# A fused attention and expert kernel in which the second dense product is folded into its neighbours

## The chip, the cores and the metric

The kernel runs on one core of a Trainium2 chip. The metric is the time of one execution in microseconds (us). A core has five engines that run side by side, each in the order of its own queue: TensorE (PE; its weight loads are listed apart as PEld), VectorE (DVE), ScalarE (ACT), GpSimd (POOL) and SyncE (SP), which here only issues transfers to the core's 16 DMA engines. ACT issues a few transfers too.

## What is computed

Attention with two head mixes gives `x` (1792 tokens x 768). Behind it stand a dense stage and a soft mixture of experts:

```python
h = x @ w_in                       # 1792 x 768 times 768 x 2048
g = h - np.tanh(h)
x = g @ w_out                      # 1792 x 2048 times 2048 x 768
logits = x @ phi                   # phi: 768 x 32 (8 experts, 4 slots each)
d = softmax(logits, axis=0)        # over the tokens
slot_input = (d.T @ x).reshape(8, 4, 768)
for e in range(8):
    slot_out[e] = np.maximum(slot_input[e] @ w1[e], 0.0) @ w2[e]   # w1: 768 x 1024, w2: 1024 x 768
c = softmax(logits, axis=1)
out = c @ slot_out
```

`w_in` and `w_out` come as 64-bit floats, all else in 32 bits. All large products run in a two-part form: an operand is split into a high part (`F32R`) and the rest, and hi*hi, lo*hi and hi*lo are added up.

## The kernel before, in words

The program is written in one order by hand (a manual schedule): each engine takes its instructions in the order in which the code issues them, and the waits follow from the data and from the buffers. `talking_heads` does the attention and, beside it, turns the 64-bit weights into 32 bits and stores them in DRAM, in 16 pieces `wi` and 16 pieces `wo` of 128 x 768. `moe_and_slots` is everything behind. Its first two products run beside the end of the attention.

Its main loop has 64 steps `t`, four batches `b` of 448 tokens times 16 slices `f` of 128 hidden units. Step `t` does

- `stage1` (L677): 18 matmuls of 128 x 448 into `hp`, slice `f` of `h` transposed (hidden units on the partitions);
- `gate`: three operations of ACT (L689 to L691) and six of DVE (L692 to L697) that make `g` of `hp`; `ready2` splits `g` (L645 on ACT, L646 on POOL or DVE);
- `stage2` (L710): 18 matmuls of 128 x 448 that add slice `f`'s share of `g @ w_out` to six banks `acc`, one or two steps later.

In batch 0 the weights come in one part and are split on the way: `split_to` makes the high part on ACT (L625) and the rest on POOL (L626), for `wi` and for `wo`; ACT's queue then stores both parts (`wis`, `wos`, 768 KB each). From batch 1 on both parts are loaded, 768 KB of `wis` and 768 KB of `wos` a step, into three and two buffers.

When `acc` of a batch is full, in the first four steps of the next one, the `prep_` functions copy it out (`x2T`), make the logits (L727), turn `x2T` by 24 transposes (L742), mix and exponentiate (L753, L756, L772) and add up the slots' inputs in `SA` (L821, L823). `sip` (L958) then gives the inputs `siT` of the experts. `hidden` (L980), `finish` (L997) and `slot_out` (L1008) run the eight experts from `w1` and `w2`; these come in 32 loads of 1536 KB (`ex`, L581) through SP's queue. SP issues them in the order of a list, each when a buffer of the list of free ones is there; a buffer comes back when PE has used it. The order ends with the second halves of `w2` of the experts 6 and 7. `slot_mix` and `output` (L1066) write the result.

Of the kernel before, what the change touches and what calls it, by code (L numbers as in the profile page):

```python
# [520 lines left out]
def moe_and_slots(tc, ident, xd, wi, wo, wis, wos, phi, w1, w2, out, box):  # L521
# [11 lines left out]
    LAG = 4  # L533
    LG = 3
    steps = [(b, f) for b in range(NB) for f in range(NF)]
    NST = len(steps)
# [4 lines left out]
    mids = ExitStack()
    firsts = ExitStack()
    keep = whole.enter_context(tc.tile_pool(name="m_keep", bufs=1))
    gp = mids.enter_context(tc.tile_pool(name="m_g", bufs=2, reuse_waits="tile"))
    temps = ExitStack()
    gt_p = temps.enter_context(tc.tile_pool(name="m_t", bufs=2, reuse_waits="tile"))
# [13 lines left out]
    queue += [4 * e + i for i in (2, 3) for e in (NE - 2, NE - 1)]  # L560

    def open_experts(stack, name, n, side):
        pool = stack.enter_context(tc.tile_pool(name=name, bufs=1, side=side, reuse_waits="tile"))
        for i in range(n):
            free.append((pool, f"{name}{i}"))

    def load_expert():
        if not queue or not free:
            return
        t = queue.pop(0)  # L570
        pool, tag = free.pop(0)
        e, part = divmod(t, 4)
        x = pool.tile([128, EXB], FP32, tag=tag, name="ex")
        i = part % 2
        if part < 2:
            n = KD // 2
            src = w1[e, i * n * 128:(i + 1) * n * 128, :]
        else:
            n = KF1
            src = w2[e, :, i * HALF:(i + 1) * HALF]  # L580
# [576 lines left out]
```

## Time and profile before

| | |
|---|---|
| median of 3 runs | 1144.0 us (1139.09 to 1148.11) |
| the profiled execution's own time | 1142.92 us |
| its span, first to last instruction | 1141.2 us |
| PE busy | 1078.0 us (94%) |
| DVE, ACT, POOL busy | 622.3, 556.4, 359.9 us |
| transfers | 274.35 MB, mean 240 GB/s |

The time of an execution is 1.7 us longer than the span of its trace. The busy share of an engine is a mean over stages that differ: in the attention, in the main loop and behind it different things come last, so the chain of what ended last (each piece followed back to what released it) and tables by stage tell more. Matmuls are pipelined: the trace gives one of 128 x 448 some 365 ns, but the next starts about 200 ns after it, so a run of them is read from start to start.

### The profile page before, as it was taken

The numbers are of one execution on the slowest core, as the hardware profiler recorded it, in microseconds if no ns is written. First come the engines' busy times: TensorE is split into PE (matmuls) and PEld (weight loads), VectorE is DVE, ScalarE is ACT, GpSimd is POOL, SyncE is SP. The second block draws the span as 40 slices with busy tenths as digits, with TensorE's granted clock in tenths as the row PEclk, the third lists the DMA queues.
The fourth block names the chain that finished last, engine by engine and source line by source line (L and its number), as shares of the span: only waits on it lengthen the run. The fifth ranks groups of instructions, "written<-read, shape, count | busy, mean of one in ns | idle before, by whom it ended". The sixth has DMA issues, their size and how long they took to land.

```text
span 1141.2 us, 20616 instructions
## 1 busy us (share of the span) xinstructions
PE 1078.0 (94%) x7400; PEld 865.1 (76%) x7400; DVE 622.3 (55%) x1330; ACT 556.4 (49%) x1245; POOL 359.9 (32%) x534
## 2 busy tenths in 40 slices
PE   8999999999989999989899999999999999998994
PEld 5677777777767777768777879997899979995452
DVE  3566576666756576645666774445634573444013
ACT  4776676766756677654344442333323342322022
POOL 1444455444634455554343301111121102110000
PEclk9999999999989999999989999999999999998999
DMA  5895678856875576447867846898465637948998
GB/s 127 236 248 172 189 217 236 225 170 181 236 211 168 180 225 218 166 165 258 293 267 277 318 166 231 302 405 326 165 236 212 238 139 271 389 170 305 379 388 310
DMA packets 158329, 274.35 MB, mean 240 GB/s; under 512 B 58292, under 2 KB 126964, under 8 KB 157716
## 3 DMA queue, kind: packets, MB, share of 16 engines
q1 hardware_dynamic: 153312, 247.76, 65.6%
q10 hardware_dynamic: 4868, 25.18, 5.5%
q8 instruction: 60, 0.98, 0.4%
q14 instruction: 41, 0.34, 0.1%
q0 software_dynamic: 48, 0.10, 0.0%
HBM read 185.71 MB, written 48.76 MB: 205 GB/s over the span
## 4 chain that ended last, share of the span: by engine, by line
PE 44%; DMA 3%; POOL 2%; issue 2%; ACT 2%; DVE 1%; ACTq 0%; POOLq 0%; SPq 0%; DVEq 0%
PE hp L677 18%; PE acc L710 18%; PE h L980 2%; PE so L1008 2%; DMA ex<-in_moe_w_dram 1%; DMA wo<-wos 1%; POOL wi L626 1%; PE tz L997 1%; POOL wo L626 1%; PE xtp L742 1%; PE lgp L727 1%; PE op L1066 1%; DMA xr<-xd 1%; ACT wi L625 1%; PE sp L821 1%
## 5 line engine op out<-in xcount | busy, mean ns | idle before, releaser
L677 PE MATMUL hp<-xh,wi 128*128 128x448 f32 x768 | 225.8, 374 | 14.2 <-POOL wi L626 9.7
L333 PEld LDWEIGHTS tm<-wk,e 120*112 120x112 f32 (+1 forms) x1440 | 176.6, 179 | 75.3 <-issue 59.6
L710 PE MATMUL acc<-gh,wo 128*128 128x448 f32 x768 | 218.5, 366 | 2.4 <-DMA wo<-wos 2.4
L299 DVE TENSOR_REDUCE mx<-pm 120x1 f32<-120x448 f32 x180 | 111.9, 622 | 138.1 <-PE pm L297 137.4
L333 PE MATMUL tm<-wk,e 120*112 120x120 f32 (+1 forms) x1440 | 179.4, 268 | 3.7 <-POOL wk L323 3.6
L297 PE MATMUL pm<-D,wpre 120*120 120x448 f32 x360 | 176.7, 573 | 1.8 <-ACT e L306 1.1
L323 POOL TENSOR_SCALAR wk<-wpost,rv 120x120 f32<-120x120 f32 x180 | 130.2, 723 | 142.1 <-PE tm L333 117.2
L677 PEld LDWEIGHTS hp<-xh,wi 128*128 128x128 f32 x768 | 145.3, 191 | 33.6 <-POOL wi L626 13.2
L336 ACT ACTIVATE aT<-tm 112x480 f32<-112x480 f32 x180 | 105.3, 585 | 125.4 <-PE tm L333 120.1
L646 POOL TENSOR_TENSOR gl<-g,gh 128x448 fp32r<-128x448 f32 x48 | 55.4, 1155 | 320.6 <-ACT gh L645 257.0
L710 PEld LDWEIGHTS acc<-gh,wo 128*128 128x128 f32 x768 | 144.0, 188 | 14.9 <-ACT xh L659 2.0
L692 DVE SCALAR_TENSOR_TENSOR qd<-qd,sq 128x448 f32<-128x448 f32 x64 | 47.2, 737 | 192.5 <-ACT qd L690 192.3
L677 PE MATMUL hp<-xl,wi 128*128 128x448 f32 x384 | 142.0, 370 | 1.3 <-DVE xl L660 1.3
L710 PE MATMUL acc<-gl,wo 128*128 128x448 f32 x384 | 140.3, 365 | 0.0
L306 ACT ACTIVATE e<-pm,mx 120x448 f32<-120x448 f32 x180 | 113.8, 632 | 4.9 <-DVE mx L299 2.6
L645 ACT ACTIVATE gh<-g 128x448 fp32r<-128x448 f32 x64 | 36.8, 576 | 138.4 <-DVE g L697 112.6
L275 ACT ACTIVATE S<-sc 120x448 f32<-120x448 f32 (+1 forms) x186 | 90.8, 544 | 13.4 <-PE sc L267 6.7
L351 PE MATMUL vx<-aT,vn 112*64 112x120 f32 (+1 forms) x1536 | 84.8, 264 | 5.2 <-DVE klo L234 5.0
L351 PEld LDWEIGHTS vx<-aT,vn 112*64 112x64 f32 x1536 | 74.9, 138 | 11.6 <-PE qx L247 6.2
L267 PE MATMUL sc<-khi,qT 64*120 64x448 f32 (+1 forms) x384 | 75.2, 385 | 6.5 <-DVE qT L251 6.1
L689 ACT ACTIVATE sq<-hp 128x448 f32<-128x448 f32 x64 | 34.5, 539 | 92.5 <-PE hp L677 72.8
L677 PEld LDWEIGHTS hp<-xl,wi 128*128 128x128 f32 x384 | 73.1, 190 | 7.8 <-DVE xl L660 2.0
(131 smaller groups left out, 1413.0 us busy)
## 6 DMA issues: line engine op xcount, KB each, us to landing
ex<-in_moe_w_dram SPq DMA_DIRECT2D x32, 1536.0 KB
wi<-wis SPq DMA_DIRECT2D x48, 768.0 KB
wo<-wos SPq DMA_DIRECT2D x48, 768.0 KB
D<-S SPq DMA_DIRECT2D x172, 210.0 KB
f<-in_moe_w_in_dram SPq DMA_DIRECT2D x32, 384.0 KB
f<-in_moe_w_out_dram SPq DMA_DIRECT2D x32, 384.0 KB
wis<-wi ACTq DMA_DIRECT2D x16, 768.0 KB
wos<-wo ACTq DMA_DIRECT2D x16, 768.0 KB
```

Source lines behind the costliest of these rows:

```text
L267: nc.tensor.matmul(xs[e][:ni], lhsT=qT[n][s, l, p, :ni], rhs=kt[s], start=(i == 0), stop=(i == 2))
L275: nc.scalar.activation(out=dst, in_=xs[e][:ni], func=ACTF.Copy)
L297: nc.tensor.matmul(x[:r], lhsT=wpre[:r, :m, :], rhs=D_t.pop(s)[:r], start=True, stop=True)
L299: nc.vector.tensor_reduce(out=mx[:r], in_=x[:r], op=ALU.max, axis=AX.X, negate=True)
L306: nc.scalar.activation(out=e[:r], in_=pp_t.pop(s)[:r], func=ACTF.Exp, bias=mx_t.pop(s)[:r], accum_out=ss[:r])
L323: nc.gpsimd.tensor_scalar(out=wk[:r], in0=wpost[:r], scalar1=ss_t.pop(s)[:r], scalar2=None, op0=ALU.mult)
L333: nc.tensor.matmul(x[:, c, :, :m], lhsT=e[:r, c * JP:(c + 1) * JP], rhs=wk[:r, :, :m], start=True, stop=True)
L336: nc.scalar.activation(out=attn_t[n][:, :, :, c0:c0 + m], in_=x[:, :, :, :m], func=ACTF.Copy)
L351: nc.tensor.matmul(x[64 * e:64 * e + 64, i, :ni], lhsT=nat_v[b, h // NP][:, h % NP, c, :], rhs=a[:, c, h, :ni], start=(c == 0), stop=(c == ...
L646: (nc.gpsimd if steps[t][0] else nc.vector).tensor_tensor(out=l, in0=src, in1=bits(h), op=ALU.subtract)
L677: nc.tensor.matmul(hp, lhsT=w[:, i, cs], rhs=x, start=(n == 0), stop=(n == 3 * KD - 1))
L710: nc.tensor.matmul(acc[c], lhsT=w[:, j, cs], rhs=g, start=(f == 0 and i == 0), stop=(f == NF - 1 and i == 2))
```

## The change

The product `g @ w_out` is no longer formed. The logits are `g @ (w_out @ phi)`, and the slots' inputs are `(d.T @ g) @ w_out`.

- `stage2`, the splitting of `g` and of `wo`, the store `wos` and its loads are gone, as are `x2T` and its transposes.
- In batch 0, each piece of `w_out` is loaded, turned by six transposes (`turn_w`), copied out by DVE and ACT, and multiplied by `phi` (`fold`, six matmuls of 32 columns), which gives a piece of `wphi`.
- In each step the slice of `g` made two steps before is turned by four transposes (`turn_g`) into a bank, and ACT copies it to a buffer by tokens. At every fourth step `logits` issues four matmuls (32 columns by 448) that add the last four slices' share.
- `gate` has a fourth operation on ACT (`mk`, for which DVE had the comparison L696) and five on DVE; `sq` now lies in PSUM. The gate of slice `t-1` is issued within the product of slice `t`, and the other pieces between the groups of three matmuls of a product (`hooks`).
- For each batch `slot_sum` makes `d.T @ g`, four groups of 512 columns, in the steps 4 to 7 of the next batch.
- Behind the loop 16 matmuls (`dt`) turn the sum over the batches, and 32 (`si`) multiply it by `w_out`, whose 16 pieces have been loaded again.
- The buffers are laid out anew. The loop's own ones leave room for 8 of the list's loads within the loop: the four loads of `w_out` (four pieces each) and the first two of `w1` in batch 1, two more of `w1` in batch 3. The other 28 loads of experts follow the loop.

```diff
...
+    def give(x, last=False):
+        free.append((x, last))
+        load_expert()
+    def load_expert():
+        if not queue or not free:
+            return
+        key = queue.pop(0)
+        home = free.pop(0)
+        x = home[0]
+        kind, t = key
+        if kind == "o":
+            for i in range(NG):
+                nc.sync.dma_start(out=x[:, i * DM:(i + 1) * DM], in_=wo[t * NG + i])
+        else:
+            e, part = divmod(t, 4)
+            i = part % 2
+            if part < 2:
+                n = KD // 2
+                src = w1[e, i * n * 128:(i + 1) * n * 128, :]
+            else:
+                n = KF1
+                src = w2[e, :, i * HALF:(i + 1) * HALF]
+            nc.sync.dma_start(
+                out=x.rearrange("p (a f) -> p a f", a=n), in_=src.rearrange("(a p) f -> p a f", p=128))
+        ex_tiles[key] = home
...
+    def load_w(t):
         if t < NST:
+            if t < NF:
+                nc.sync.dma_start(out=ring[t % 3][:, 1], in_=wi[t])
             else:
+                nc.sync.dma_start(out=ring[t % 3], in_=wis[t % NF])
+    def split_w(t):
         if t < NF:
+            w = ring[t % 3]
+            nc.scalar.activation(out=r32(w[:, 0]), in_=w[:, 1], func=ACTF.Copy)
+            nc.gpsimd.tensor_tensor(out=r32(w[:, 1]), in0=w[:, 1], in1=w[:, 0], op=ALU.subtract)
+    def save_w(t):
+        if t < NF:
+            nc.scalar.dma_start(out=wis[t], in_=ring[t % 3])
...
+    def product(t, hooks):
+        b, f = divmod(t, NF)
+        hp = bank(f"h{t % 3}", [128, SEQ], "hp")
+        w = r32(ring[t % 3])
         for c in range(KD):
+            for fn in hooks.get(c, []):
+                fn()
             cs = slice(c * 128, (c + 1) * 128)
+            for i, (hl, l) in enumerate(((0, 0), (1, 0), (0, 1))):
+                nc.tensor.matmul(
+                    hp, lhsT=w[:, hl, cs], rhs=r32(x_of(b, c, l)),
+                    start=(c == 0 and i == 0), stop=(c == KD - 1 and i == 2))
+        hps[t] = hp
+        for fn in hooks.get(KD, []):
+            fn()
+    def gate_act(t):
+        hp = hps[t]
+        qd, th, mk = mem["t"][GR:GR + 3]
+        sq = bank(f"q{t % 2}", [128, SEQ], "sq")
+        mem["sq"] = sq
         nc.scalar.activation(out=sq, in_=hp, func=ACTF.Square)
         nc.scalar.activation(out=qd, in_=sq, func=ACTF.Square, bias=tshift)
+        nc.scalar.activation(out=th, in_=hp, func=ACTF.Tanh)
+        nc.scalar.activation(out=mk, in_=sq, func=ACTF.Relu, bias=tlimit, scale=-1.0)
+    def gate_first(t):
+        hp, sq = hps[t], mem["sq"]
+        qd, th, mk = mem["t"][GR:GR + 3]
         nc.vector.scalar_tensor_tensor(out=qd, in0=qd, scalar=TG_E, in1=sq, op0=ALU.add, op1=ALU.mult)
+        nc.vector.tensor_tensor(out=mem["t"][t % GR], in0=hp, in1=th, op=ALU.subtract)
+        nc.vector.scalar_tensor_tensor(out=th, in0=sq, scalar=-TG_A, in1=qd, op0=ALU.add, op1=ALU.mult)
+    def gate_last(t):
+        hp = hps.pop(t)
+        qd, th, mk = mem["t"][GR:GR + 3]
+        nc.vector.scalar_tensor_tensor(out=hp, in0=th, scalar=TG_C, in1=hp, op0=ALU.mult, op1=ALU.mult)
+        nc.vector.copy_predicated(out=mem["t"][t % GR], mask=mk.bitcast(I32), data=hp)
...
-    def stage2(t):
...
-        for c in range(KD):
-            cs = slice(c * 128, (c + 1) * 128)
-            for i, (j, g) in enumerate(((0, gh), (1, gh), (0, gl))):
-                nc.tensor.matmul(
-                    acc[c], lhsT=w[:, j, cs], rhs=g, start=(f == 0 and i == 0), stop=(f == NF - 1 and i == 2))
...
+    turns = [0]
+    def turn_bank(shape, name):
+        turns[0] += 1
+        return bank(f"r{turns[0] % 2}", shape, name)
+    def turn_g(t):
+        b, f = divmod(t, NF)
+        if f % NG == 0:
+            tok[b, f // NG] = quads.pop(0)
+        g = mem["t"][t % GR]
+        x = turn_bank([JP, NR, 128], "gt")
+        for r in range(NR):
+            nc.tensor.transpose(out=x[:, r, :], in_=g[:, r * JP:(r + 1) * JP], identity=ident)
+        i = f % NG
+        dst = tok[b, f // NG][:JP].rearrange("p (r f) -> p r f", r=NR)[:, :, i * 128:(i + 1) * 128]
+        nc.scalar.activation(out=dst, in_=x, func=ACTF.Copy)
+    def load_o(f):
+        if f < NF:
+            nc.sync.dma_start(out=mem["wo"][f % 4], in_=wo[f])
+    def turn_w(f, hf):
+        x = turn_bank([128, HALF], "wt")
+        for i in range(KD // 2):
+            c = hf * (KD // 2) + i
+            nc.tensor.transpose(
+                out=x[:, i * 128:(i + 1) * 128], in_=mem["wo"][f % 4][:, c * 128:(c + 1) * 128], identity=ident)
+        dst = mem["wt"][f % 2][:, hf * HALF:(hf + 1) * HALF]
+        if hf:
+            nc.scalar.activation(out=dst, in_=x, func=ACTF.Copy)
+        else:
+            nc.vector.tensor_copy(out=dst, in_=x)
+    def fold(f):
+        x = turn_bank([128, NSL], "wp")
         for c in range(KD):
+            nc.tensor.matmul(
+                x, lhsT=mem["wt"][f % 2][:, c * 128:(c + 1) * 128], rhs=phs[:, c, :],
+                start=(c == 0), stop=(c == KD - 1))
+        nc.vector.tensor_copy(out=wphi[:, f, :], in_=x)
...
+    def logits(b, k):
+        if k == 0:
+            lg[b] = bank("lg", [128, SEQ], "lgp")
+        for g in range(NG):
+            f = k * NG + g
+            nc.tensor.matmul(
+                lg[b][NSL * g:NSL * g + NSL, :], lhsT=wphi[:, f, :], rhs=mem["t"][(b * NF + f) % GR],
+                start=(k == 0), stop=(k == NQ - 1))
...
+    def slot_sum(b, k, x):
+        a, es = es_in[b]
+        n = tok.pop((b, k))
+        for r in range(NR):
+            nc.tensor.matmul(
+                x[NSL * r:NSL * r + NSL, :], lhsT=es[:, r, :], rhs=n[:JP, r * FB:(r + 1) * FB], start=True, stop=True)
+        quads.append(n)
+        s = mem["SA"][:, k * FB:(k + 1) * FB]
+        if b:
+            nc.vector.scalar_tensor_tensor(out=s, in0=s, scalar=a, in1=x, op0=ALU.mult, op1=ALU.add)
+        else:
+            nc.vector.tensor_copy(out=s, in_=x)
+    folds = {}
+    for f in range(NF):
+        folds.setdefault(f + 3 if f < 2 else f + 2 if f < 7 else f + 1, []).append(f)
+    def step(t):
+        b, f = divmod(t, NF)
+        hooks = {}
+        def on(c, fn, *a):
+            hooks.setdefault(c, []).append(lambda: fn(*a))
+        load_w(t + 2)
+        for n in folds.get(t - 1, []):
+            load_o(n + 4)
+        if t == 2:
+            gate_act(0)
+            gate_first(0)
+            gate_last(0)
+        gate_act(t - 1)
+        u = t - 2
+        for n in folds.get(t, [])[:1]:
+            on(1, turn_w, n, 0)
+        on(1, gate_first, t - 1)
+        on(5 if t == 2 else 2, turn_g, u)
+        for n in folds.get(t, [])[1:]:
+            on(2, turn_w, n, 0)
+        for n in folds.get(t, [])[:1]:
+            on(3, turn_w, n, 1)
+        if b == 0:
+            on(3, split_w, t + 1)
+            on(1, save_w, t)
+        if b and f == 1:
+            on(3, logits, b - 1, NQ - 1)
+            on(4, logits_out, b - 1)
+        if b and f == 2:
+            hooks[1] = [lambda: mix_t(b - 1), lambda: slot_exp(b - 1)] + hooks[1]
+            on(3, mix_n, b - 1)
+            on(KD, slot_run, b - 1)
+            on(KD, gates_first, b - 1)
+        if b and f == 3:
+            on(4, slot_turn, b - 1)
+            on(KD, gates_last, b - 1)
+        if b and 4 <= f < 4 + NQ:
+            on(3, lambda k: slot_sum(b - 1, k, turn_bank([128, FB], "sp")), f - 4)
+        on(4, gate_last, t - 1)
+        if b + 1 < NB:
+            if f == 6:
+                load_x(b + 1)
+            if 8 <= f < 8 + KD:
+                on(4, split_x, b + 1, f - 8)
+        for n in folds.get(t, [])[1:]:
+            on(4, turn_w, n, 1)
+        for n in folds.get(t, []):
+            on(KD - 1, fold, n)
+        if u % NG == NG - 1 and u % NF < NF - 1:
+            on(KD, logits, u // NF, u % NF // NG)
+        product(t, hooks)
+        if b == 1 and f % 2 == 1 and f // 2 < NX:
+            give(mem["ex"][f // 2], f // 2 == NX - 1)
+        if b == NB - 1 and f in (1, 3):
+            if f == 1:
+                mem["xz"] = xap.tile([128, 2 * EXB], FP32, tag="xa", name="xz")
+            give(mem["xz"][:, f // 2 * EXB:(f // 2 + 1) * EXB])
+    for t in range(3):
+        load_w(t)
+        if t == 0:
+            load_x(0)
...
+    for t in range(2, NST):
+        step(t)
+    t = NST
     b = NB - 1
+    rz = rxp.tile([128, 3 * RU + XW], FP32, tag="rx", name="rz")
+    for i in range(3):
+        give(rz[:, i * EXB:(i + 1) * EXB])
+    gate_act(t - 1)
+    gate_first(t - 1)
+    turn_g(t - 2)
+    gate_last(t - 1)
+    turn_g(t - 1)
+    logits(b, NQ - 1)
+    logits_out(b)
+    give(tq[:, :EXB])
+    mix_t(b)
+    slot_exp(b)
+    slot_turn(b)
+    slot_run(b)
+    dgs = [bank(n, [128, FB], "sp") for n in ("h0", "h1", "q0", "q1")]
+    sr = keep.tile([128, NSL], FP32, tag="sr", name="sr")
+    rv = keep.tile([128, 1], FP32, tag="rv", name="rv")
     nc.vector.tensor_scalar(out=rv, in0=run_s, scalar1=EPS, scalar2=None, op0=ALU.add)
     nc.vector.reciprocal(out=rv, in_=rv)
     nc.vector.tensor_scalar(out=sr, in0=seld, scalar1=rv, scalar2=None, op0=ALU.mult)
+    dt = bank("h2", [128, NF, NSL], "dt")
+    for k in range(NQ):
+        slot_sum(b, k, dgs[k])
+    for f in range(NF):
+        nc.tensor.matmul(dt[:, f, :], lhsT=mem["SA"][:, f * 128:(f + 1) * 128], rhs=sr, start=True, stop=True)
+    for i in range(1, 4):
+        give(tq[:, i * EXB:(i + 1) * EXB])
+    dgT = wphi
+    nc.scalar.activation(out=dgT[:, :NF // 2], in_=dt[:, :NF // 2], func=ACTF.Copy)
+    nc.vector.tensor_copy(out=dgT[:, NF // 2:], in_=dt[:, NF // 2:])
+    si = [bank(f"r{hf}", [128, HALF], "si") for hf in range(2)]
+    for k in range(NQ):
+        w = take(("o", k), NG)
+        for hf in range(2):
+            for g in range(NG):
+                nc.tensor.matmul(
+                    si[hf][NSL * g:NSL * g + NSL, :], lhsT=dgT[:, k * NG + g, :],
+                    rhs=w[:, g, hf * HALF:(hf + 1) * HALF], start=(k == 0), stop=(k == NQ - 1))
+        load_expert()
+    tt = tq[:, 4 * EXB:]
+    siS = mem["SA"][:, :DM]
+    nc.vector.tensor_copy(out=siS[:, :HALF], in_=si[0])
+    nc.scalar.activation(out=siS[:, HALF:], in_=si[1], func=ACTF.Copy)
+    sp = bank("h0", [128, KD, NSL], "sip")
     for c in range(KD):
+        nc.tensor.matmul(sp[:, c, :], lhsT=siS[:, c * 128:(c + 1) * 128], rhs=seld, start=True, stop=True)
+    siT = tt[:, 2 * FH:2 * FH + KD * NSL].rearrange("p (c s) -> p c s", c=KD)
     nc.scalar.activation(out=siT, in_=sp, func=ACTF.Copy)
+    mix_n(b)
...
```

Three places show how the queues change.

PE in batch 1, 2 or 3 where one batch ends and the next begins before the change (`hp` and `acc` are the two products, `lgp` the logits, `xtp` the transposes):

```order
L710 MATMUL acc<-gh,wo 128x448 x2
L710 MATMUL acc<-gl,wo 128x448
L677 MATMUL hp<-xh,wi 128x448 x2
L677 MATMUL hp<-xl,wi 128x448
L727 MATMUL lgp<-x2T,phs 32x448 x6
L742 MATMUL xtp<-ident,x2T 112x128 x12
```

and within a batch with it (`gt` is the turned `g`):

```order
L705 MATMUL gt<-ident,tq 112x128 x4
L662 MATMUL hp<-rx 128x448 x12
L741 MATMUL lgp<-tq,wphi 32x448 x4
L662 MATMUL hp<-rx 128x448 x6
L705 MATMUL gt<-ident,tq 112x128 x4
L662 MATMUL hp<-rx 128x448 x18
```

The 18 matmuls of `acc` are gone from each step; four transposes stand in their place, and the logits have moved from the batch's end into every fourth step.

ACT in a step of batch 0, before:

```order
L625 ACTIVATE wi<-wi 128x768
L689 ACTIVATE sq<-hp 128x448
L690 ACTIVATE qd<-sq,tshift 128x448
L691 ACTIVATE g<-hp 128x448
L625 ACTIVATE wo<-wo 128x768
L645 ACTIVATE gh<-g 128x448
L632 DMA wis_108<-wi 128x1536
L632 DMA wos_123<-wo 128x1536
```

and with the change (`tq` holds the gate's buffers and `g` by tokens, `ex` the turned piece of `w_out`, `rx` the pieces of `w_in`):

```order
L674 ACTIVATE sq<-hp 128x448
L675 ACTIVATE tq<-sq,tshift 128x448
L676 ACTIVATE tq<-hp 128x448
L677 ACTIVATE tq<-sq,tlimit 128x448
L635 DMA wis_111<-rx 128x1536
L708 ACTIVATE tq<-gt 112x4x128
L722 ACTIVATE ex<-wt 128x384
L630 ACTIVATE rx<-rx 128x768
```

One split of a weight is left instead of two, and it stands behind the gate and the two copies of what PE has turned.

SP at the end of the loop, before:

```order
L619 DMA wo<-wos_131 128x1536
L619 DMA wo<-wos_132 128x1536
L581 DMA ex<-in_moe_w_dram 128x3x1024
L581 DMA ex<-in_moe_w_dram 128x8x384 x2
L581 DMA ex<-in_moe_w_dram 128x3x1024 x2
```

and with the change (`rz`, `tq`, `ex` and `xz` are all homes of expert weights here):

```order
L625 DMA rx<-wis_115 128x1536
L625 DMA rx<-wis_116 128x1536
L605 DMA rz<-in_moe_w_dram 128x8x384 x2
L605 DMA rz<-in_moe_w_dram 128x3x1024
L605 DMA tq<-in_moe_w_dram 128x3x1024
L605 DMA tq<-in_moe_w_dram 128x8x384 x2
```

Behind the last piece of weights 21 expert loads are queued before, 28 with the change.

## Rows read from the trace of the kernel before

**Rows 1.** Busy time by stage: stretch, length, each engine (instructions), clock, DMA share, GB/s

```profile
525.00:661.00 136.00, 122.27 (x578) 107.57 (x575) 89.32 (x116) 57.80 (x96) 53.66 (x29) 0.96 0.76 286
...
787.00:914.00 127.00, 126.42 (x650) 113.92 (x649) 65.78 (x124) 43.49 (x84) 18.48 (x16) 1.00 0.58 211
...
1055.00:1103.00 48.00, 46.44 (x448) 23.16 (x444) 3.48 (x10) 7.59 (x19) 1.56 (x5) 0.96 1.03 381
```

**Rows 2.** The chain that ended last, batches 1 to 3: start, length, what

```profile
664.92 1.63 PE lgp L727 x12
666.56 1.45 PE xtp L742 x12
...
671.66 0.76 PE lT L753 x2
672.41 0.72 PE ln L756 x8
...
706.67 3.65 PE acc L710 x18
710.32 3.65 PE hp L677 x18
```

**Rows 3.** The same chain at the loop's start and in batch 0

```profile
525.74 3.85 PE hp L677 x18
...
542.51 5.29 PE hp L677 x17
...
605.18 0.85 ACT wi L625
...
606.10 1.82 POOL wi L626
...
607.97 3.71 PE hp L677 x17
...
624.50 3.71 PE hp L677 x17
```

**Rows 4.** ACT within one step of batch 1, in order of time (start, length)

```profile
743.19 0.54 ACT L689 ACTIVATE sq<-hp 128x448 f32<-128x448 f32 x1 [2.00 <-PE hp L677]
...
744.34 0.53 ACT L691 ACTIVATE g<-hp 128x448 f32<-128x448 f32 x1
```

**Rows 5.** DVE within the same step: its gate's first and last two operations

```profile
744.47 0.63 DVE L692 SCALAR_TENSOR_TENSOR qd<-qd,sq 128x448 f32<-128x448 f32 x1 [3.95 <-ACT qd L690]
...
746.73 0.39 DVE L696 TENSOR_SCALAR sq<-sq 128x448 f32<-128x448 f32 x1
747.15 0.66 DVE L697 COPY_PREDICATED g<-sq,hp 128x448 f32<-128x448 int32 x1
```

**Rows 6.** Groups of instructions by line and shape: busy us, mean ns, idle before

```profile
L336 ACT ACTIVATE aT<-tm 112x480 f32<-112x480 f32 x172 | 100.8, 586 | 110.9 <-PE tm L333 105.5 <-PE vx L351 4.9
...
L660 DVE TENSOR_TENSOR xl<-xr,xh 128x448 fp32r<-128x448 f32 x24 | 17.5, 789 | 0.8 <-ACT xh L659 0.7
```

**Rows 7.** The chain behind the loop: start, length, what

```profile
1077.02 2.58 PE so L1008 x32
1079.60 1.88 PE tz L997 x16
...
1103.29 15.82 DMA ex<-in_moe_w_dram
...
1119.15 1.50 PE so L1008 x16
```

**Rows 8.** Transfers by line (page): one load of experts

```profile
ex<-in_moe_w_dram SPq DMA_DIRECT2D x32, 1536.0 KB
```

**Rows 9.** Three short stretches: columns as in rows 1

```profile
542.50:547.80 5.30, 5.29 (x18) 4.76 (x19) 4.22 (x7) 1.31 (x2) 1.49 (x1) 0.68 0.81 298
...
920.20:921.60 1.40, 1.40 (x16) 1.40 (x14) 1.26 (x3) 0.96 (x2) 0.80 (x1) 1.00 0.82 325
...
1047.80:1050.20 2.40, 2.35 (x12) 2.28 (x12) 0.39 (x2) 0.00 (x0) 0.00 (x0) 0.59 1.02 410
```

More of the change, by code (lines that the diff above doesn't have):

```diff
@@ L532, in moe_and_slots @@
     FH = F1 // 2
[L533 to L536, printed above, removed]
+    NST = NB * NF
     EXB = KD * F1 // 2
     OG = 4
-    whole = ExitStack()
[L541 to L546, printed above, removed]
@@ L560, in moe_and_slots @@
[L560 to L580, printed above, removed]
-        nc.sync.dma_start(
-            out=x.rearrange("p (a f) -> p a f", a=n), in_=src.rearrange("(a p) f -> p a f", p=128))
-        ex_tiles[t] = (x, pool, tag)
@@ new lines, in moe_and_slots @@
+    rx = rxp.tile([128, 3 * RU + XW], FP32, tag="rx", name="rx")
+    xa = xap.tile([128, 2 * EXB], FP32, tag="xa", name="xa")
+    ring = [rx[:, i * RU:(i + 1) * RU].rearrange("p (h i) -> p h i", h=2) for i in range(3)]
+    xbuf = [xa, rx[:, 3 * RU:]]
+    free, ex_tiles, kept_homes = [], {}, []
+    queue = [("o", k) for k in range(NQ)] + [("e", 0), ("e", 1)]
+    for e in range(NE - 1):
+        queue += [("e", 4 * e + 4), ("e", 4 * e + 5)]
+        if e < NE - 2:
+            queue += [("e", 4 * e + 2), ("e", 4 * e + 3)]
@@ L606, in load_i, with take, take_expert @@
+    def take(key, n):
+        home = ex_tiles.pop(key)
+        if home[1]:
+            kept_homes.append(home[0])
+        else:
+            free.append(home)
+        return home[0].rearrange("p (a f) -> p a f", a=n)
+    def take_expert(t, n):
+        return take(("e", t), n)
+    def load_w(t):
         if t < NST:
[L607 to L612 removed]
@@ L844, in moe_and_slots @@
     for i in range(0, KD, 2):
-        split_x(0, range(i, i + 2))
+        for c in range(i, i + 2):
+            split_x(0, c)
         if i == 0:
-            split_i(0)
+            split_w(0)
         yield
-    hps = {0: stage1(0)}
-    load_i(2)
-    split_i(1)
+    product(0, {})
+    split_w(1)
     yield
-    gate(0, hps[0])
-    hps[1] = stage1(1)
-    save()
-    load_i(3)
-    split_i(2)
+    product(1, {})
+    save_w(0)
+    load_w(3)
+    split_w(2)
+    save_w(1)
     while not box.get("go"):
@@ new lines, in moe_and_slots @@
+    for tag in ("h2", "q0", "q1", "r0", "r1", "lg"):
+        bank_pool[tag] = acc
+    mids = whole.enter_context(tc.tile_pool(name="m_mid", bufs=1, side="right", reuse_waits="tile"))
+    tq = mids.tile([128, TW + (NQ + 1) * FB * NR], FP32, tag="tq", name="tq")
+    mem["SA"] = mids.tile([128, NF * 128], FP32, tag="SA", name="SA")
+    mem["ex"] = [mids.tile([128, EXB], FP32, tag=f"ex{i}", name="ex") for i in range(NX)]
+    mem["t"] = [tq[:, i * SEQ:(i + 1) * SEQ] for i in range(GR + 3)]
+    mem["wo"] = [mem["ex"][0][:, i * DM:(i + 1) * DM] for i in range(4)]
```

387 lines of the change are left out of this document (92 added, 295 removed).

## The prediction

> **What bounds the kernel now.** I read the table by stage first, then the chain of what ended last in each stage, then the timelines of the engines beside it. In the batches 1 to 3 PE is busy nearly without a gap, 126.4 of 127 us, at full clock [rows 1], and the chain consists of runs of `hp` and `acc`, 3.65 us each [rows 2]: a step costs 7.30 us, 0.203 us a matmul, and everything else hides. In batch 0 the pace is another: from one run of `hp` to the like one two steps later 16.53 us pass (607.97 to 624.50), 8.3 us a step, and between stand the splits of weights, 0.85 us on ACT and 1.82 us on POOL, for which the product waits [rows 3]. Behind the loop DMA comes last: it moves 381 GB/s with its engines busy all the time [rows 1], 21 loads of experts stand in SP's queue behind the loop's last weights, and PE waits for one of them for 15.8 us of the chain [rows 7]. So three stages have three limits, and the change touches all of them. The attention, which ends with the first `hp` of the loop at 525.74 us [rows 3], is left as it is.
>
> **The steps of the batches 1 to 3.** Out go 18 matmuls of `acc`, 3.65 us a step [rows 2]. In come four transposes of the shape that `xtp` has, 12 of which take 1.45 us [rows 2]: 0.121 us each, 0.48 us. The logits come in every fourth step: four matmuls of 32 columns, which the trace lists as eight. The nearest row is `so`, also of 32 columns in four groups side by side: 32 pieces of 384 columns in 2.58 us [rows 7], so 0.081 us each, 0.094 us at 448 columns, 0.76 us for the four slices, 0.19 us a step. By `lgp`, with three groups, they would cost 0.136 us each [rows 2], 0.27 us a step; I take `so`, which has the same four groups. A step has 3.65 + 0.48 + 0.19 = 4.32 us of PE.
>
> Does PE stay the limit? ACT's gate now lasts from 743.19 to 744.87 us [rows 4], 1.68 us; a fourth operation makes it 2.3 us, and the copy of the turned `g` (512 columns; 480 take 0.586 us [rows 6]) 2.9 us. DVE's gate runs from 744.47 to 747.81, 3.34 us, less the comparison's 0.42 us (746.73 to 747.15) [rows 5]: 2.92 us. Six steps of a batch add a split of `x` (0.79 us [rows 6]), four a slot sum (estimate 0.7 us, from the same row): 3.7 us at most. Both are below 4.32. The path through them is longer: `hp` is read some 0.2 us after the next product has begun (one matmul's pitch), DVE follows ACT's start by 1.28 us [rows 4, 5], and `g` is there after 0.2 + 1.28 + 2.92 = 4.4 us. `turn_g` wants it after six matmuls of the product behind, at 4.32 + 1.2 = 5.5 us. It is covered by 1.1 us; without this cover PE would wait by the excess in each of 48 steps.
>
> The weights need 0.79 MB in 4.32 us, 182 GB/s, of 381. In batch 1 six loads of the list (1.57 MB each [rows 8]) and 1.38 MB of `x` fall into twelve steps: with the weights 20.2 MB in 57 us, 355 GB/s. That is close, and I allow 4 us for late weights (bounds 0 and 12, the latter one load of three per pair of steps in a row).
>
> Once a batch PE also has `lT` 0.76 and `ln` 0.72 us [rows 2], a small transpose of some 0.35 us (four pieces, less than 0.121 us each), and the slot sums, 32 listed pieces of 512 columns, 0.107 us each by `so`: 3.4 us. That is 5.3 us; the old batch end (`lgp`, two `xtp`, `lT`, `ln` and more) cost some 7 us and goes. Sum: 48 x 4.32 + 3 x 5.3 + 4 = 227 us, and 2 us for the last `fold`, which falls into batch 1: 229 us. Before, three batches took 377 us (661 to 1038 us).
>
> **Batch 0.** PE's step has 4.32 us as above, six transposes of `w_out` (0.73 us) and `fold`, six matmuls of few columns, twelve listed, of which `tz` has 16 in 1.88 us [rows 7]: 1.41 us. That is 6.46 us. The other path: ACT's gate until 2.5 us, the two copies until about 3.9 (with the issue of a store between), the split 0.85, POOL 1.82 [rows 3]: 6.6 us, and the next product's second matmul waits for it. The two paths tie; I take 6.7 us, with bounds 6.5 and 8.3 (the pace before, if the order on ACT goes worse than counted). The loop's first product starts at 525.74, but the gate of slice 0 now stands behind the attention, so it ends at about 531.3: 4.4 us for `g`, 0.5 for its turn, 0.6 for three matmuls. Then 13 steps of 6.7 us and two more folds in steps that have two (2.1 us each): batch 1 starts at 531.3 + 87.1 + 4.3 = 622.7 us, where it had been 661, and the loop ends at 852.
>
> **Behind the loop** more is left to load: 28 loads instead of 21, since only four expert loads fit into the loop. PE needs about 30 us for the sums up to `siT` and then some 7 us an expert (`h`, 2.58 + 1.88 us and waits, [rows 7]), 90 us in all; 27 loads of 1.573 MB at 381 GB/s take 111.5 us. Three homes are free at once (12 us of loading), one more after the logits, three after the slot sums (some 15 us), four while `si` runs, so I see no gap in the stream: DMA sets the end. Before, the last but one load freed `so` at 1119.15 us [rows 7], 22.0 us before the end of the span, and the order behind it is the same. With 1.5 us for the first to start: 852 + 1.5 + 111.5 + 22 = 987 us of span, and 1.7 us around it: **989 us**, against 1142.9 of the profiled execution (which lies 0.1% below the median). The loop gives back 186 us, the tail takes some 32 of them.
>
> The DMA price can be read otherwise. The stretch shows 381 GB/s over 48 us with engines that are always busy [rows 1], a short one beside it 410 GB/s [rows 9], by which the 27 loads take 103.6 us. I take the long one, since the tail is long. The Trainium skill (Perfetto Trace Analysis, Roofline) puts the 16 DMA engines of a core at about 435 GB/s together. By that figure the loads would take 97.7 us and the time would be 975 (an estimate); no stretch of this trace comes up to it.
>
> **The rivals.** (1) ACT and DVE do not overlap as counted, because each gate waits for the buffers of the one before, and their 2.3 + 2.9 = 5.2 us set the step: 48 x 0.9 = 43 us more, 1032. Against it: DVE starts 1.28 us behind ACT, not 2.3 [rows 4, 5]. (2) Late weights. A piece can be loaded only when the product three before it has ended, two steps before its use; if each takes 10 us from that point, a step is 5 us, and the time 989 + 33 = 1022. For it: in batch 1 other loads stand ahead in the queue; against it: a piece alone needs 2.1 us at 381 GB/s. (3) DMA moves 410 GB/s through the whole tail [rows 9]: 8 us less, 981. (4) **Slower than before**: PE's clock falls in the loop. After a wait the granted clock is 0.68 and 17 `hp` take 5.29 us instead of 3.71 [rows 3, 9], so at 1.2 GHz the work takes twice as long as at 2.4 (estimate from the ratio). The new steps mix transposes into the products; if these kept the clock at 1.2 GHz, the loop's 225 us of PE in batches 1 to 3 would become 450, and batch 0's 84 some 168: 1,290 us, and it passes the time before once half of the loop runs so. Against it: the stretch of 12 transposes between products has clock 1.00 [rows 9]. The Trainium skill (TensorE: Matmul & The Clock Gate, Part 4) says that the full rate does not engage for transposes in PE's transpose mode, which would speak for this rival; in these rows they run at it, among matmuls. (5) The tail gives everything back: it would need 28 loads at 165 GB/s, less than half of the row. That is the case of no change.
>
> **How the numbers follow.** The forecast 0.72, (1) 0.10, (2) 0.08, (3) 0.05, (4) 0.03, (5) 0.02. Low end: batch 0 at 6.5 us a step (-3), no late weights (-4), DMA at 410 (-8): 974, and 972 with the fold in batch 1 hidden (-2). High end: batch 0 at 8.3 (+21), logits by `lgp` (+4), late weights (+8) and the like: 1022; I go to 1035 for (1). A measurement of this kernel tells about 1% from no change. Faster 0.95, the same 0.02, slower 0.03.
>
> **What would show it.** In the profile after: runs of 18 `hp` and four `gt` with a period of 4.3 to 4.4 us and the clock at 1.00; 6.5 to 7 us in batch 0 with POOL's split as what the product waits for; the loop's end near 850; behind it 28 loads at about 380 GB/s, with PE waiting for them. The prediction is wrong if PE waits for DVE or ACT before each `gt`, if `hp` waits for `wis`, or if the stream of loads breaks while homes are awaited.

## The result, and the profile after

The changed kernel takes 1000.5 us (median of 4 runs, 997.8 to 1005.1), the kernel before beside it 1141.6 us: a ratio of 0.876, 95% interval [0.871, 0.882]. It is faster by 12.4%; the forecast of 989 us was 11.5 us too low. The profiled execution took 999.17 us with a span of 997.5 us.

The table by stage, with the columns of [rows 1]: batch 0, batches 1 to 3, and two stretches behind the loop.

```profile
532.00:622.00 90.00, 88.55 (x584) 77.71 (x585) 58.81 (x103) 53.22 (x99) 22.04 (x13) 1.00 0.77 260
622.00:704.00 82.00, 81.04 (x459) 65.06 (x457) 57.36 (x103) 48.96 (x96) 0.00 (x0) 1.00 0.80 291
704.00:783.00 79.00, 77.84 (x433) 61.99 (x432) 57.04 (x102) 47.08 (x93) 0.00 (x0) 1.00 0.53 179
783.00:860.00 77.00, 75.36 (x418) 59.56 (x416) 52.91 (x95) 42.23 (x84) 0.00 (x0) 1.00 0.50 180
860.00:900.00 40.00, 31.70 (x254) 15.27 (x258) 11.09 (x27) 6.98 (x16) 0.56 (x2) 0.83 0.94 345
900.00:960.00 60.00, 48.38 (x408) 23.06 (x400) 3.28 (x9) 6.65 (x17) 1.87 (x6) 0.88 1.05 390
```

PE is still the busiest engine of the loop, at clock 1.00, but with larger gaps: 1.2 us are missing in 79, where 0.6 were in 127 [rows 1]. A batch takes 78.6 us (from one `lT` to the next, 633.20 to 711.80) where it had 126 to 128. Batch 0 takes 6.2 us a plain step (the time from one run of `gt` to the next) where it had 8.3. Behind the loop DMA works at its limit again, with a lower rate in the first 40 us.

Where the 1.2 us go, the chain of what ended last shows (start, length, what), here over one step of batch 2, in place of the `hp` and `acc` that alternated in [rows 2]:

```profile
744.64 0.54 ACT sq L674
...
746.27 0.53 ACT tq L677
746.81 0.02 issue
746.83 0.62 DVE tq L682
...
749.34 0.68 DVE tq L690
750.02 0.14 issue
750.15 0.62 PE gt L705 x4
750.77 2.44 PE hp L662 x12
753.21 0.89 PE lgp L741 x8
```

In this step no piece of PE is in the chain for 5.5 us: it runs through all four operations of ACT's gate, then through DVE's five, and PE comes back with `gt`. In [rows 4, 5] DVE began 1.28 us behind ACT's first operation; here it begins 2.19 us behind it, when the fourth (L677, `mk`) has ended. The waits of the batches 1 to 3 (in total, times, longest) say the same of DVE, and how little of it reaches PE:

```profile
DVE tq L682 <- ACT tq L677: 56.9, 40, 2.4
...
PE gt L705 <- DVE tq L690: 2.1, 9, 0.3
```

PE's tail, by its timeline (start, length, what; in brackets the wait in front):

```profile
864.81 1.07 PE L705 MATMUL gt<-ident,tq 128*112 128x128 f32 x4 [3.49 <-DVE tq L690]
...
872.86 6.03 PE L817 MATMUL sp<-tq,es 112*32 112x512 f32 x32 [0.37 <-ACT es L810]
...
975.81 1.50 PE L1037 MATMUL so<-xz,tq 128*32 128x384 f32 x16 [0.27 <-DMA xz<-in_moe_w_dram]
```

The same table for three stretches in between, DMA's rate last:

```profile
866.00:870.00 4.00, 3.34 (x10) 0.51 (x4) 0.00 (x0) 1.06 (x2) 0.00 (x0) 0.50 1.08 382
874.00:878.00 4.00, 4.00 (x24) 0.91 (x20) 1.50 (x2) 0.00 (x0) 0.00 (x0) 0.53 0.78 309
878.00:882.00 4.00, 4.00 (x41) 3.18 (x29) 1.49 (x2) 0.00 (x0) 0.56 (x2) 1.00 0.39 118
```

PE waits 3.49 us for the last gate, its clock falls to 0.50 (1.2 GHz), and the slot sums take 6.03 us. Three of the tail's loads wait for these sums, since their homes hold the turned `g`: DMA falls to 309 and then 118 GB/s. Against 390 GB/s that is (81 + 272) x 4 us = 1.41 MB, 3.6 us of the stream. The last load but one frees `so` at 975.81, 21.7 us before the end, as before (22.0, [rows 7]).

### The profile page after: what moved, and what is told of

It is laid out like the page before. It is cut to its first block, busy times and chain, and to the rows that moved or that the text cites. A ratio compares the mean times of both kernels' runs of the same rounds, so it can differ in the third digit from the quotient of the medians.

```text
span 997.5 us, 19368 instructions
## 1 busy us (share of the span) xinstructions
PE 932.4 (93%) x6936; PEld 699.3 (70%) x6936; DVE 572.4 (57%) x1260; ACT 569.4 (57%) x1287; POOL 273.3 (27%) x471
## 4 chain that ended last, share of the span: by engine, by line
PE 72%; DMA 11%; DVE 7%; ACT 6%; issue 2%; SPq 1%; POOL 1%; ACTq 0%; POOLq 0%; DVEq 0%
PE hp L662 18%; PE pm L297 13%; PE tm L333 12%; PE vx L351 7%; PE sc L267 7%; DMA xz<-in_moe_w_dram 3%; PE gt L705 2%; DMA ex<-in_moe_w_dram 2%; PE wp L729 2%; PE sp L817 2%; DMA tq<-in_moe_w_dram 2%; PE lgp L741 2%; DMA kn<-in_k_dram 1%; DMA D<-S 1%; DVE tq L684 1%
## 5 line engine op out<-in xcount | busy, mean ns | idle before, releaser
L662 PE MATMUL hp<-xa,rx 128*128 128x448 f32 x576 | 141.6, 383 | 1.5 <-POOL rx L631 1.4
L662 PE MATMUL hp<-rx 128*128 128x448 f32 x576 | 132.7, 376 | 0.0
L662 PEld LDWEIGHTS hp<-rx 128*128 128x128 f32 x576 | 104.1, 188 | 20.8 <-issue 13.3
L662 PEld LDWEIGHTS hp<-xa,rx 128*128 128x128 f32 x576 | 101.7, 190 | 19.0 <-issue 7.0
L1019 POOL MEMSET tq<- 128x256 f32 x8 | 2.4, 311 | 340.4 <-PE sp L817 263.1
L682 DVE SCALAR_TENSOR_TENSOR tq<-tq,sq 128x448 f32<-128x448 f32 x64 | 39.7, 620 | 69.0 <-ACT tq L677 69.0
L312 POOL TENSOR_SCALAR rv<-ss 120x1 f32<-120x1 f32 x180 | 41.8, 232 | 111.4 <-ACT e L306 101.0
L297 PEld LDWEIGHTS pm<-D,wpre 120*120 120x120 f32 x360 | 51.7, 183 | 25.4 <-ACT e L306 11.8
L67 POOL TENSOR_TENSOR fa<-fa,f 128x384 f32<-128x384 f32 x64 | 65.2, 1019 | 5.4 <-issue 0.4
L267 PEld LDWEIGHTS sc<-khi,qT 64*120 64x120 f32 (+1 forms) x384 | 41.5, 171 | 20.4 <-PE tm L333 5.8
```

Source lines behind the costliest of these rows:

```text
L67: eng.tensor_tensor(out=out, in0=bits(a), in1=bits(p), op=ALU.add)
L267: nc.tensor.matmul(xs[e][:ni], lhsT=qT[n][s, l, p, :ni], rhs=kt[s], start=(i == 0), stop=(i == 2))
L297: nc.tensor.matmul(x[:r], lhsT=wpre[:r, :m, :], rhs=D_t.pop(s)[:r], start=True, stop=True)
L312: nc.gpsimd.tensor_scalar(out=rv[:r], in0=ss_t.pop(s)[:r], scalar1=EPS, scalar2=None, op0=ALU.add)
L662: nc.tensor.matmul(hp, lhsT=w[:, hl, cs], rhs=r32(x_of(b, c, l)), start=(c == 0 and i == 0), stop=(c == KD - 1 and i == 2))
```

## The experiments

The attention ahead of the loop ends some microseconds earlier or later in each execution. Where traces are compared, three lengths are used: from the loop's second `gt` to the end of the span; **batch 0** from there to the first `lT`; **tail** from the last `gt` but one to the end. The changed kernel has 463.8, 99.5 and 136.8 us.

**The changed kernel again**, unaltered.

> The changed kernel as it is, for a time beside the others on one chip. Both theories: 1000 us (996 to 1005), batches 1 to 3 in 238 us.

1002.8 us (998.2 to 1004.6), 0.877 [0.874, 0.880]; the lengths are 465.2, 100.0 and 137.4, a batch 78.8 us. The lengths of the two traces differ by 0.5 to 1.4 us; a single difference of that size shows nothing.

**mk behind DVE's first operations (e1).**

```diff
...
     def gate_act(t):
...
-        nc.scalar.activation(out=mk, in_=sq, func=ACTF.Relu, bias=tlimit, scale=-1.0)
     def gate_first(t):
...
         nc.vector.scalar_tensor_tensor(out=th, in0=sq, scalar=-TG_A, in1=qd, op0=ALU.add, op1=ALU.mult)
+        nc.scalar.activation(out=mk, in_=sq, func=ACTF.Relu, bias=tlimit, scale=-1.0)
```

> The fourth operation of ACT's gate (mk) stands behind DVE's first three in the program, so that DVE's first waits for qd alone; no engine's order changes. Theory A (DVE starts 0.9 us late because it waits for mk, g is ready about 5.6 us after the start of the next product, and so each plain step takes 4.4 to 4.5 us where PE has 4.09 us of work): DVE starts 1.2 to 1.3 us after ACT, g comes 0.9 us earlier, PE stops waiting before gt, the three batches fall from 238 to 227 to 230 us, and the time to 988 to 992 us. Theory B (PE's own work is dearer than counted, and its waits are small things of other kinds): no change, 998 to 1002 us.

1009.0 us, 0.885 [0.882, 0.887]: slower than the changed kernel, which neither theory had. Yet a batch fell from 78.8 to 77.15 us, as theory A had it, and the loss is in batch 0: 115.4 us, 16 more, 7.5 us a plain step. The timeline of batch 0 (start, length, what, wait) shows why:

```profile
562.13 0.63 ACT L684 ACTIVATE tq<-sq,tlimit 128x448 f32<-128x448 f32 x1 [2.71 <-DVE tq L683]
...
564.44 1.83 POOL L631 TENSOR_TENSOR rx<-rx 128x768 fp32r<-128x768 f32 x1 [5.95 <-ACT rx L630]
...
566.32 0.68 PE L662 MATMUL hp<-xa,rx 128*128 128x448 f32 x2 [0.61 <-POOL rx L631]
```

Now `mk` waits for DVE, 2.71 us. Behind it in ACT's queue stand the copies and the split of the next weights, behind the split POOL, behind POOL the product. The expectation had looked at DVE alone and not at what is queued behind the moved operation.

**mk behind only from batch 1 on (e1b).** The same edit under `if t >= NF`.

> mk stands behind DVE's first three operations only from batch 1 on; batch 0 keeps the order of the changed kernel. Theory A (in batch 0 the later mk held up ACT's copies and the split of weights behind it; in the batches 1 to 3 the shorter path was a gain): batch 0 goes back to about 90 us (6.2 us a plain step), a batch of 1 to 3 takes 76.7 to 77.2 us instead of 78.8, and the time is 994 to 997 us. Theory B (the later mk costs ACT time everywhere): 1000 us or more.

997.2 us, 0.873 [0.871, 0.876]. Batch 0 is back at 100.1 us, a batch takes 77.15 us, and DVE begins 1.25 us behind ACT, released by `qd` and no longer by `mk`, as two rows of a plain step show:

```profile
701.61 0.55 ACT L677 ACTIVATE sq<-hp 128x448 f32<-128x448 f32 x1
...
702.86 0.62 DVE L686 SCALAR_TENSOR_TENSOR tq<-tq,sq 128x448 f32<-128x448 f32 x1 [0.85 <-ACT tq L678]
```

Theory A held (its range ended at 997): both halves of the former result are explained.

**The turn of g later in the product (e8).**

```diff
-        on(5 if t == 2 else 2, turn_g, u)
+        on(5 if t == 2 else 4 if b else 2, turn_g, u)
```

> From batch 1 on the turn of g stands after the twelfth matmul of a product instead of the sixth, 1.2 us later; the gate is left as it is. Theory A (a path from the product through ACT and DVE that is too long for its cover by some 0.3 us in plain steps): the cover grows by 1.2 us and holds, the same 988 to 992 us as with the shorter path. Theory B (PE's own prices): 998 to 1002 us. Theory C (ACT or DVE is at its limit of work, and not a path through both): a later turn moves the wait, 998 to 1004 us.

993.6 us, 0.870 [0.868, 0.873]; 459.0 us in the trace, 4.8 to 6.2 less than the two traces of the changed kernel. A batch takes 76.7 us, and PE has no gap left in the like stretch of the table:

```profile
704.00:783.00 79.00, 79.00 (x445) 64.47 (x444) 58.60 (x104) 49.07 (x94) 0.00 (x0) 1.00 0.53 185
```

DVE still starts behind `mk` here, so the path is as long as before and only its cover has grown. Theory A held in its mechanism, but the time is 1.6 us above its range (and 4.4 below the others'): 2.1 us a batch, and the rest of the miss lies elsewhere. Four steps took 17.94 us and now take 17.46.

**Matmuls in PE's waits behind the loop (e12)**, on the identity, into an unused bank:

```diff
...
     turn_g(t - 2)
+    keep_busy(26)
     gate_last(t - 1)
     turn_g(t - 1)
     logits(b, NQ - 1)
     logits_out(b)
     give(tq[:, :EXB])
+    keep_busy(5)
     mix_t(b)
     slot_exp(b)
+    keep_busy(12)
     slot_turn(b)
+    keep_busy(3)
...
```

> 46 matmuls of 128 columns on the identity, whose result nobody reads, stand in PE's waits just behind the loop (26, 5, 12 and 3 of them), where the clock now falls to 0.50 and the slot sums take 6.03 us; the loads behind the loop have a gap of some 6 us there, as three homes wait for these sums. Theory A (loads set the end of the tail, and the gap counts): the clock stays near 1.00, sp takes 3.1 to 3.5 us, the gap shrinks by 3 to 5 us, and the time falls by as much, 995 to 997 us. Theory B (the gap is made up later, since PE's own work or the homes set the end): 999 to 1001 us. Theory C (the added matmuls only delay the real ones): 1001 to 1004 us.

1001.1 us, 0.877 [0.874, 0.880], no change. The clock stayed at 1.00 up to the slot sums and `sp` took 3.64 us, but the added matmuls overran the waits they were to fill, the 26 most of all:

```profile
862.89 5.97 PE L948 MATMUL spin<-ident 128*128 128x128 f32 x52
868.69 0.60 PE L705 MATMUL gt<-ident,tq 128*112 128x128 f32 x4
```

5.97 us stood in a wait of 3.5, so most of what the clock gave was spent ahead of it: the slot sums end 17.3 us after the last `gt` but one, where it was 18.2. That is theory C in part; the time alone would also fit theory B, and the next run tells them apart.

**Fewer of them, with the later turn (e8w).** As e8, with 5 (ahead of the first `turn_g`), 14, 2, 7 and 1.

> The later turn of g together with matmuls on the identity in PE's waits behind the loop, fewer than before (5, 14, 2, 7 and 1), so that they fill the waits and do not overrun them. Theory A (the gap in the loads counts, and 46 matmuls were some 2 us too long): the clock stays near 1.00 up to the slot sums, these end about 3 us earlier after the loop's end than without, and the time is 990 to 992 us. Theory B (what is gained there waits for the next home of the loads): 993 to 994 us, as with the later turn alone.

991.8 us, 0.868 [0.866, 0.870]. The median is 1.9 us below that of e8 and the intervals overlap; the trace tells more. The tail fell from 137.1 to 132.2 us, but the `gt` from which it is counted came 1.1 us later here, since five matmuls stand ahead of it:

```profile
854.84 1.38 PE L948 MATMUL spin<-ident 128*128 128x128 f32 x10 [1.35 <-DVE tq L690]
856.06 0.60 PE L705 MATMUL gt<-ident,tq 128*112 128x128 f32 x4
...
865.42 3.64 PE L817 MATMUL sp<-tq,es 112*32 112x512 f32 x32
```

From the end of the last product on, 134.8 us are left instead of 138.6, 3.8 less, and the slot sums end 15.6 us after it instead of 19.7 (in e8 PE stood still for 1.45 us there, up to its `gt` at 857.09). The stream runs without a gap at 375 to 410 GB/s from 858 us on, as the table by stretches of the same kernel shows for two of them:

```profile
866.00:870.00 4.00, 4.00 (x41) 1.67 (x31) 2.99 (x4) 0.00 (x0) 0.56 (x2) 1.00 1.03 410
870.00:874.00 4.00, 3.53 (x29) 3.39 (x31) 0.06 (x1) 0.38 (x1) 0.00 (x0) 0.73 1.03 375
```

Theory A: the 3.8 us are about the gap (3.6), which counted in full, and a low clock of PE had lengthened a stage that DMA bounds.

**Two more loads behind the loop (e2, e2c).** First the two loads that batch 3 issues were written ahead of the loop's following ones:

> The two loads of w1 that batch 3 issues are issued behind the loop instead, so that 30 loads stand there in place of 28. Theory A (the stream of loads sets the end of the tail): two loads of 1.573 MB at 385 GB/s, 8.2 us more, 1007 to 1011 us. Theory B (PE's work or the homes set the end): 999 to 1003 us.

1000.9 us, 0.876 [0.873, 0.878], no change; but it tested nothing. SP's timeline has the two loads here:

```profile
842.95 0.96 SPq L605 DMA_DIRECT2D xz<-in_moe_w_dram  x2
...
856.02 2.95 SPq L605 DMA_DIRECT2D rz<-in_moe_w_dram  x3
```

SP had no work left, came to the loads 13 us before the loop's end, and their home had long been free. So they were put behind loads that do wait:

```diff
...
     for i in range(1, 4):
         give(tq[:, i * EXB:(i + 1) * EXB])
+    xz = xap.tile([128, 2 * EXB], FP32, tag="xa", name="xz")
+    for i in range(2):
+        give(xz[:, i * EXB:(i + 1) * EXB])
...
```

> The changed kernel with the two loads of w1 that batch 3 issues put into SP's queue behind the first seven loads of the tail, so that they can't start during the loop, as they did when they stood first behind it (SP ran ahead and issued them 13 us before the loop's end). Theory A (the stream of loads sets the tail's end): 3.15 MB more at 385 GB/s behind the loop, 8.2 us more, the last wait for a load 8 us later, 1007 to 1011 us. Theory B (PE or the homes set the end): 998 to 1003 us.

1010.9 us, 0.887 [0.885, 0.889]. The tail is 145.6 us, 8.2 more than in the repeat of the changed kernel. Theory A: each load counts in full, 4.1 us.

**Batch 0 without the folds (e4).**

> Left out: the turns of w_out and the folds with phi in batch 0 (wphi holds a constant instead). It takes 2 us of PE and two copies out of most steps of batch 0. Theory A (PE and the path through ACT's copies, its split and POOL tie at 6.2 us, so that the path through the split sets the pace once PE has less): a step of 5.6 to 5.8 us, 6 to 8 us less in all, 993 to 996 us. Theory B (PE alone sets the pace of batch 0): a step of 4.2 to 4.5 us, 26 us less, 974 to 977 us.

975.6 us, 0.855 [0.852, 0.857]. (With the folds 12 of the 16 loads of `w_out` in batch 0 are gone too; nothing waited for them.) Batch 0 fell by 24.5 us (75.0), nearly theory B's sum, but by theory A's mechanism: a step takes 5.05 us, not 4.2 to 4.5, and the waits of 52 us of batch 0 (in total, times, longest) name the split:

```profile
PE hp L662 <- POOL rx L631: 5.2, 7, 1.1
```

So the path through the split sets 5.05 us once ACT has no copy of `w_out` ahead of it; 5.6 to 5.8 had been expected. It is a closed circle, as the chain shows: the split, POOL's part, five matmuls of the product that waited for it, and `gt`, whose copy (0.49 us) stands ahead of the next split:

```profile
592.87 0.85 ACT rx L630
...
593.79 1.84 POOL rx L631
...
595.68 1.27 PE hp L662 x5
596.95 0.44 PE gt L705 x4
```

In the changed kernel PE itself never waits for POOL in the plain steps, but its weight load does by a hair, as this row of the repeat's timeline shows:

```profile
563.33 0.30 PEld L662 LDWEIGHTS hp<-xa,rx 128*128 128x128 f32 x2 [0.20 <-POOL rx L631]
```

Those 0.20 us are what a plain step (6.2 us) has above the sum of PE's pieces (6.01), so the two paths tie to 0.2 us there: PE is busy for 88.55 of 90 us, and the split comes just as late.

**A cheaper fold, and an earlier split (e15, e16)**, on top of e8w:

```diff
...
             nc.tensor.matmul(
-                x, lhsT=mem["wt"][f % 2][:, c * 128:(c + 1) * 128], rhs=phs[:, c, :],
+                x[NSL * g:NSL * g + NSL, :], lhsT=phs[:, c, :], rhs=mem["wt"][f % 2][:, c * 128:(c + 1) * 128],
...
+    def fold_sum(f):
+        x = turn_bank([128, NSL], "wq")
+        nc.tensor.matmul(x, lhsT=mem["ws"][f % 2], rhs=seld, start=True, stop=True)
+        nc.vector.tensor_copy(out=wphi[:, f, :], in_=x)
...
```

> The later turn of g and the matmuls in the tail's waits as before, and two edits in batch 0: the fold multiplies phi (32 columns as weights, four groups side by side) by the turned w_out, 128 columns at a time, and one more matmul adds the groups up and turns the result; and the split of the next weights stands ahead of the gate in ACT's queue. Theory A (in batch 0 PE's fold and the path through the split tie at 6.2 us a plain step, and both get shorter): 5.6 to 5.9 us, 983 to 987 us. Theory B (the six matmuls of a fold cost as much in either form, and PE's work sets the step): 990 to 993 us. Theory C (the split in front holds up the gate): above 994 us.

1004.6 us, 0.880 [0.877, 0.883], theory C in another way. The fold's twelve pieces take 0.56 us in the chain instead of 1.26, but the split that stood first waits for its weights, and the gate behind it with it:

```profile
577.09 0.84 ACT L630 ACTIVATE rx<-rx 128x768 fp32r<-128x768 f32 x1 [6.33 <-DMA rx<-wi]
...
580.53 0.69 PE L718 MATMUL wt<-ident,ex 128*128 128x128 f32 x2 [4.12 <-ACT tq L708]
```

In the second try the split stands behind the gate and only ahead of the copy of `w_out`:

> As the kernel with the new fold, the later turn of g and the matmuls in the tail's waits, but the split of the next weights goes back behind the gate in ACT's queue, only ahead of ACT's copy of the turned w_out instead of behind it. Theory A (the split in front was held by weights that had not landed and held the gate; with the split 0.5 us earlier than in the changed kernel and 0.4 us less of PE a fold, batch 0 is faster): plain steps of 5.6 to 5.9 us, batch 0 some 5 to 9 us shorter, 982 to 987 us. Theory B (the weights land too late for the earlier split, or the wait for the new fold's copy eats the gain): 990 us or more.

988.4 us, 0.865 [0.861, 0.869]; 452.1 us in the trace, 2.6 less than e8w. This is the fastest version that leaves nothing out, 12 us below the changed kernel, though its interval overlaps that of e8w. Batch 0 gained 3.0 us, not 5 to 9: plain steps take 5.74 us as expected in its first half, but 6.5 us where the next batch's `x` is split, since DVE's part of that stands ahead of the copy that the new matmul waits for:

```profile
582.31 1.24 DVE L648 TENSOR_TENSOR rx<-rx 128x448 fp32r<-128x448 f32 x1
...
583.80 0.41 PE L737 MATMUL wq<-seld,ex 128*128 128x32 f32 x2 [0.49 <-DVE ex L733]
```

**The kernel before with a third of its second product (e6).**

```diff
...
-            for i, (j, g) in enumerate(((0, gh), (1, gh), (0, gl))):
+            for i, (j, g) in enumerate(((0, gh),)):
...
```

> The kernel before with one of the three matmuls per bank in the second product (hi*hi alone; lo*hi and hi*lo are left out), all else as it was: 6 matmuls of acc a step instead of 18. Theory A (in the batches 1 to 3 PE's matmuls alone set the pace, in batch 0 the split of weights): 48 steps lose 2.43 us each, batch 0 little, 1020 to 1035 us. Theory B (the gate, the splits of g or the weights stand close behind PE, so that much of what the change gave came from their leaving and not from the matmuls): a step stays above 6 us, 1080 us or more.

1076.2 us, 0.944 [0.941, 0.947], between the theories and nearer to B. From the first `lT` to that of the last batch 307 us pass instead of 369, 62 less; PE lost 48 x 2.43 = 117 us of work. Most of the rest became waits, for weights and for the gate above all; from 660 to 960 us PE's waits add up to 37 us:

```profile
PE hp L677 <- DMA wi<-wis: 12.4, 7, 2.6
PE acc L710 <- DMA wo<-wos: 6.1, 4, 1.8
PE hp L677 <- DVE sq L696: 5.7, 2, 2.9
```

The clock, 1.00 in these batches before [rows 1], was 0.94 to 0.98 in this run, so that PE's own work took longer too:

```profile
740.00:820.00 80.00, 68.14 (x337) 56.88 (x335) 50.11 (x93) 30.65 (x61) 11.88 (x10) 0.95 0.80 306
```

So fewer matmuls alone give about half of what they take. The change also took half of the weights out of the loop and the split of `g` out of the path. That this let the matmuls' leaving count in full fits these waits; no run takes out the one without the other.

## Why the prediction held, and where it was short

**The loop's gain** (right). PE's time set the pace, 3.65 us of `acc` left each step, and no late weights came: a batch with expert loads (78.6 us) takes as long as one without (711.80 to 790.60, 78.8). The 4 us allowed for them were not needed, nor was rival (2).

**The step of the batches 1 to 3** (PE sets the pace as predicted; the cover and two prices were mis-sized). Predicted were 4.32 us a step and 5.3 a batch, 74.4 a batch; measured 78.7.
- *The cover of g* was counted as 1.1 us, with DVE 1.28 us behind ACT. It starts 2.19 us behind, because the fourth operation, put in by this change, stands ahead of DVE's wait. DVE's own part takes 3.2 us, 2.92 were counted. The path is 5.5 us from `sq` to `gt`. Also, 4.32 was a mean: a plain step has 3.65 + 0.44 = 4.09 us of PE and one with logits more, and a path limits each step by itself. A plain step and six matmuls (1.22 us) cover 5.3 us, some 0.2 too little: where no slot sum stands, about one step in four takes 4.47 us instead of 4.09 (680.70 to 685.17, for example). Two experiments, one that shortens the path (1.7 us a batch) and one that lengthens the cover (2.1 us), show it. Rival (1) had the place, with a price of 43 us; it was 6. It had been held unlikely by the 1.28 us of the kernel before, which the new gate did not keep.
- *PE's own prices* make up the other 2.2 us. Eight pieces of logits take 0.89 us (0.76 counted by `so`, 1.09 by `lgp`), a slot sum's eight 1.00 (0.86), and each such visit lengthens the time from `gt` to `gt` by another 0.2 us (5.18 and 5.28 against 4.09 in e8), which was in no term. 4 x 0.13 + 4 x 0.14 + 8 x 0.2 = 2.7 us, less 16 x 0.04 for `gt` (0.44 instead of 0.48): 2.0 us.

**Batch 0** (mechanism right, the sum right in part by luck). 6.7 us a step were taken, with PE's path (6.46) and the split's (6.6) in a tie. Plain steps take 6.2, below the lower bound of 6.5; but the three with logits take 7.2, a second fold in a step adds 2.7 (2.1 counted) and the first of the 13 steps waits 1.4 us for POOL's split. These misses cancel: the 13 steps took 91.2 us (from some 530.0 to 621.2), 91.4 were predicted. That the loop's batch 1 began 1.5 us early (621.2 for 622.7) comes from the attention, which ended 1.9 us earlier in this execution (523.86 for 525.74). The two paths did tie, by the weight load's 0.20 us above, at 6.2 instead of 6.6 us: PE has 3.65 + 0.44 + 0.66 (turns of `w_out`) + 1.26 (fold) = 6.01 us in a plain step, and the split's path was counted 0.4 us too long.

**Behind the loop** (mechanism right, one sentence wrong). DMA sets the end, as e2c shows. The failed step is "I see no gap in the stream": homes had been counted as free "after the slot sums (some 15 us)", and at half clock these ended 19.6 us after the loop (859.3 to 878.9). The gap cost 3.6 us, and 3.8 came back when PE's clock was kept up (e8w). The rate of 381 GB/s was well taken: 390 in the long stretch. The Trainium skill (Perfetto Trace Analysis, Roofline) puts the 16 DMA engines at about 435 together; the best stretch here reached 410.

**The sum**: the loop ended 7.3 us late (859.3 for 852), the stream was 3.5 us longer than counted (975.8 - 859.3 for 113), the end 0.3 us shorter: together the 10.5 us between the span that was forecast (987) and the one measured (997.5). The 7.3 us hide more: three batches were 3 x 4.3 = 12.9 us too short in the forecast, and the 4 us for late weights that never came and the 1.5 us at the start of batch 1 made up for some of it.

**The signs.** Of the three signs of being wrong that the prediction names, one came (the stream broke while homes were awaited) and one came in part (PE waits for DVE before one `gt` in four); `hp` did not wait for `wis`.

**The clock** (rival 4) did not fall in the loop: 1.00 in every stage of it, with four transposes among 18 matmuls. The Trainium skill (TensorE: Matmul & The Clock Gate, Part 4), by which the full rate does not engage for transposes in transpose mode, is not borne out here for transposes among matmuls. Behind the loop, where the clock fell, PE had waited. The rival's sum was off as well (989 + 225 + 84 is 1,298, not 1,290); nothing hangs on it.
